# Eight places of a hand-written order and an earlier fetch for two chunks, in an RWKV-7 block followed by a squared-ReLU feed-forward layer

## The chip, the cores and the metric

The kernel runs on one core of a Trainium2 chip. The metric is the device time of one execution in microseconds, as the median of several runs. All products are in float32; the feed-forward weights arrive as 64-bit floats and are converted on the chip. The engines are TensorE (PE in the profile; PEld is its weight load), VectorE (DVE), ScalarE (ACT), GpSimd (POOL) and SyncE (SP), which only issues DMAs. "SPq", "ACTq" and "POOLq" are the queues from which the engines' sequencers issue.

## The reference

A linear recurrence over 768 time steps for 4 batches and 8 heads of 40 dimensions, and then a feed-forward layer over the 3072 tokens (320 to 2048 to 320):

```python
for t in range(S):
    y[:, :, t] = np.einsum('bhd,bhde->bhe', rt, state)
    Sa = np.einsum('bhde,bhe->bhd', state, at)
    state_decay = state * wt[:, :, None, :] - np.einsum('bhd,bhe->bhde', Sa, bt)
    state = state_decay + np.einsum('bhd,bhe->bhde', vt, kt)
...
x = attn_out.transpose(0, 2, 1, 3).reshape(B * S, H * D)
h = np.maximum(x @ w_in, 0.0)
return (h * h @ w_out).astype(np.float32)
```

## The kernel before

The 768 steps are cut into six pieces of 128, so with four batches there are 24 chunks, numbered 0 to 23; chunk i is piece i // 4 of batch i % 4. Chunk i needs the state left by chunk i - 4. Within a chunk the recurrence becomes matrix products and the inverse of a triangular matrix (I + N), built of a and b and the decays.

Each chunk passes through these stages:

- `early(i)`, in six steps: TensorE turns w, VectorE makes running products of it (the decays), TensorE turns b and a, VectorE scales them, TensorE multiplies them and ScalarE copies the result to the tile N. The decays go to `kept_e[i]` in device memory, N to `kept_q` or `kept_d` (what the solver reads), `kept_n` (its lower block) and, for chunks 0 to 13, `kept_m` (the two 32-row operands that join halves of an inverse).
- `take(u)` and `solving(u)`: GpSimd reads N back for a unit of one, two or four chunks (0; 1; 2-3; 4-5; 6-7; 8-9; 10-11; 12-13; 14-17; 18-21; 22-23) and solves for the inverse row by row; the result goes to `kept_t[u]`. The units up to 12-13 are "fine": they solve blocks of 32, and two 32x32 products join each pair of blocks to one of 64.
- `inverses(j)` fetches the inverse again (tile `blocks` for a fine unit, straight to T for the others), calls `arrive(j)` for N and, in a fine unit, the joins' operand (tile `spares`), and for a fine unit does the join in three further steps: VectorE turns `blocks`, TensorE multiplies with `spares`, ScalarE copies, TensorE multiplies again, ScalarE copies to T.
- `chain(i)`, in eight steps: the products with the state, with T and N, and the new state; this is the serial part. Its output is a block of tokens.
- The feed-forward layer works on two chunks' tokens at a time: `thirds` and `whole` (first product, then ScalarE's ReLU), `square` (VectorE), `make_quarter` (second product).

The schedule is written out by hand, and each engine runs its instructions in the order in which the program emits them. There are two parts. The opening is a list of words, taken one after the other (line 932): `e4.1` is step 1 of `early(4)`; `LA`, `LW`, `lk`, `lb`, `lr`, `lv` fetch a and b, w, k, b, r, v; `sE`, `sN` store decays and N; `K` and `S` take and solve a unit; `B`, `A`, `J` fetch a fine inverse, its N with the joins' operand, and do a step of the join; `D` fetches decays; `rv`, `mrv`, `k`, `a`, `kb`, `ds`, `ts` prepare a chunk; `x` begins a chain and `c` does its next step; `mv` gathers tokens; `th`, `wh`, `sq`, `q` are the feed-forward steps; `pa` and `pd` are halves of a step that converts weights (ScalarE and VectorE in turn); `W` fetches weights; and `f` with a number is filler: matmuls of the identity whose result nobody reads, that many 128x128 columns of them. `@a` and `@g` put a word's DMA on ScalarE's or GpSimd's queue; otherwise it is SyncE's.

The second part is a loop of slots 7 to 23. Slot i (`sorted_slot`) runs chunk i's chain, chunk i + 1's preparation with its inverse, and feed-forward steps; near its end `loads(i + 2)` fetches the decays, k and b of chunk i + 2, and for a chunk that is the later one of its unit (`soon`) starts `inverses` at once. For the first chunk of a fine pair, `inverses` is started at the head of the slot before its own, right behind the first `make_quarter`: its first step issues `blocks`, then `arrive`'s three DMAs. Chunks 8 and below are fetched in the opening.

`arrive` does nothing when N is already there, so a later call of `inverses` for the same chunk issues only `blocks`. Line 494 is the fetch of N, 498 that of the joins' operand, 513 that of `blocks`, 969 that of decays in the loop and 891 in the opening; 264 is the filler, 331 a turn, 87 any product, 372 to 381 the scans, 401 a copy of N, 532 and 539 the copies in a join, 561 a copy of the turned v, 658 those of `times_t` in the chain.

Of the kernel before, what the change touches and what calls it, by code (L numbers as in the profile page):

```python
# [17 lines left out]
def kernel(  # L18
# [42 lines left out]
    for h, d, n in ((6, 0, D), (7, 0, D), (5, HALF, D - HALF)):  # L61
        while n:
            j, row, room_ = free[at]
# [4 lines left out]
            d, n = d + m_, n - m_  # L68
# [23 lines left out]
    def new(name, shape, bufs):  # L92
        return work.tile(shape, FP32, tag=name, name=name, bufs=bufs)
# [7 lines left out]
    def tick():  # L101
        for entry in line:
            entry[0] -= 1
        while line and line[0][0] <= 0:
            line.pop(0)[1]()
# [12 lines left out]
    class Ring:  # L118
# [6 lines left out]
        def next(self):  # L125
            self.at = (self.at + 1) % len(self.tiles)
            return self.tiles[self.at]
# [15 lines left out]
    def fetch(ring, src, i):  # L143
        bb, c = order[i]
        t_ = rings[ring].next()
        on_queue[0].dma_start(out=t_[:, :, :D], in_=src[bb, :, c * C:(c + 1) * C, :].rearrange("h t d -> t h d"))
        return t_
# [168 lines left out]
    FINE = 8  # L316
# [3 lines left out]
    unit_of = {first + n: u for u, (first, nb) in enumerate(units) for n in range(nb)}  # L320
# [170 lines left out]
    def arrive(i, g, queue=nc.sync):  # L491
        if "N" not in g:
            g["N"] = new("N21", [HC, H, HC], 2)
            queue.dma_start(out=g["N"], in_=kept_n[i])
            if unit_of[i] < FINE:
                g["joins"] = spare("joins", i)
                for half in range(2):
                    queue.dma_start(out=g["joins"][half * HC:half * HC + Q], in_=kept_m[i][half, :, :, Q:])

    def inverses(i, g, queue=nc.sync, own_n=True):  # L500
        bb, c = order[i]
        u = unit_of[i]
        kept = kept_t[u][:, i - units[u][0]]
        g["T"] = T = new("T", [128, H, HC], 2)
        if u >= FINE:
            for col in range(classes(u)):
                queue.dma_start(out=T[col::classes(u)], in_=kept[col].rearrange("h f j t -> (f j) h t"))
        else:


            blocks = new("blocks", [128, H, Q], 1)
            for col in range(classes(u)):
                queue.dma_start(out=blocks[col::classes(u)], in_=kept[col].rearrange("h f k j t -> (f k j) h t"))
        if own_n:
            arrive(i, g, queue)
        if u >= FINE:
            return
        yield
        upper_ = spare("turned", i)
        nc.vector.transpose(upper_.rearrange("p h t -> p (h t)"), blocks.rearrange("p h t -> p (h t)"))  # L520
        for n in range(2):
            nc.scalar.activation(T[:, :, n * Q:(n + 1) * Q], blocks, Act.Copy, scale=which[:, n:n + 1])
        yield
        small = lambda: psum(ps_w)[:, :H * Q].rearrange("p (h t) -> p h t", h=H)
        p_ = small()
        mv = spare("mv", i)
        ends_ = [(slice(half * HC, half * HC + Q), slice(half * HC + Q, (half + 1) * HC)) for half in range(2)]
        for h in range(H):
            for one, two in ends_:
                mm(p_[two, h], g["joins"][one, h], upper_[one, h], True)  # L530
        for one, two in ends_:
            nc.scalar.copy(mv[two], p_[two])
        yield
        p_ = small()
        for h in range(H):
            for one, two in ends_:
                mm(p_[one, h], mv[two, h], blocks[two, h], True)
        for one, two in ends_:
            nc.scalar.copy(T[one, :, Q:], p_[one])
        yield  # L540


    soon = lambda i: i < 2 * B or unit_of[i - 1] == unit_of[i]
# [267 lines left out]
    def run(gen):  # L811
        for _ in gen:
            tick()
# [63 lines left out]
    def advance(u, n_):  # L877
        if u not in solves:
            solves[u] = [-1, solving(u, range(100), *((nc.vector, solved[:, Q * Q // 4:Q * Q // 2]) if u == 0 else ()))]
        while solves[u][0] < n_ and next(solves[u][1], "end") != "end":  # L880
            solves[u][0] += 1
        if n_ > 90:
            run(solves[u][1])
# [46 lines left out]
    }  # L930

    for word in """
e0.1 lv0 e0.2 e0.3 e0.4 e0.5 e1.1 e0.6 sN0 K0 LW2 e1.2 e1.3 e1.4 LA2 f3 e1.5 e1.6 sN1 K1 LW3 k0 a0 rv0 f2 e2.1 V0.10 V0.20 V0.31 f22 lk1 lv1 LA3 W0@g S1.8 mrv0 kb0 e2.2 e2.3 Z0 LW4 B0 e2.4 e3.1 x0 f10 e3.2 e2.5 sE2 e2.6 sN2 J0 e3.3 e3.4 J0 J0 e3.5 sE3 e3.6 sN3 c0 c0 c0 c0 c0 lv2 lr1 S1.20 c0 c0 LA4 S1.99 K2 B1 f3 W1 rv1 mrv1 lr2 f6 LW5 f4 e4.1 e4.2 e4.3 k1 kb1 e4.4 e4.5 W2@g LA5 sE4 pa0 lk2 pd0 D2 LW6 a1 e4.6 f5 pa1 pd1 x1 J1 pa2 pd2 W3 lv3 lb2 sN4 A2 pa3 pd3 rv2 f2 e5.1 e5.2 J1 f24 J1 f3 c1 LA6 S2.4 S2.99 f6 c1 mrv2 lr3 c1 f6 c1 e5.3 e5.4 e5.5 sE5@g f8 k2 c1 c1 c1 kb2 a2 pa4 e5.6 sN5@a pd4 pa5 pd5 e6.1 e6.2 x2 f30 e6.3 e6.4 B2 J2 K3 lk3 mv0 W4 A3 f10 e6.5 J2 J2 rv3 c2 c2 c2 e6.6 pa6 pd6 c2 mrv3 lb3 f9 LA7 D3 k3 pa7 B3 J3 LW7 c2 c2 kb3 lr4 sE6 J3 lv4 e7.1 pd7 pa8 c2 W5 lv5 lb4 a3 f8 lk4@a J3 e7.2 A4 rv4 W8 D4 sN6 S3.99 B4 W6 x3 W7 c3 pd8 c3 e7.3 pa9 pd9 mrv4 e7.4 e7.5 LA8 LW8 c3 pa10 J4 k4 sE7 pd10 W11 e7.6 c3 W10 lr5 c3 sN7 K4 S4.99 pa11 pd11 W12 kb4 ds4 J4 J4 pa12 pd12 c3 ts4 W9 f4 pa13 pd13 W13 a4 pa14 c3 D5 B5 mv1 pd14 e8.1 e8.2 f4 x4 lk5 W14 A5 LA9 c4 pa15 pd15 pa16 pd16 ds5 pa17 f10 rv5 pd17 f3 th0 J5 pa18 pd18 W15@a pa19 pd19 W16 lb5 mrv5 wh0 c4 pa20 pd20 pa21 lr6 c4 th0 wh0 e8.3 pd21 lv6 c4 e8.4 LA10 W17 e8.5 LW9 k5 kb5 c4 c4 e8.6 pa22 pd22 W19 sN8 th0 sE8 wh0 LW10 a5 J5 th0 wh0 sq0 W18@g pa23 ts5 c4 lk6 D6 e9.1 e9.2 A6 J5 e9.3 e9.4 e9.5 x5 lb6 B6 c5 f1 sq0 sE9@a pd23 W20 e9.6 sN9 K5 LW11 rv6 lv7 LA11 pa24 ds6 e10.1 e10.2 c5 pd24 pa25 mrv6 pd25 e10.3 k6 J6 pa26 pd26 c5 th0 wh0 e10.4 LA12 e10.5 sE10 lr7 c5 c5 th0 J6 kb6 c5 c5 e11.1 a6 ts6 e10.6 sN10 LW12 LW13 lk7@a e11.2 mv2 wh0 D7 e11.3 x6 e11.4 J6 q0 sq0 q0 e11.5 e12.1 e11.6 sN11@g S5.99 K6 S6.99 e12.2 sq0 e12.3 q0 q0 c6 B7 lb7 sE11 rv7 A7 wh0 q0 c6 mrv7 e12.4 q0 ds7 q0 J7 e12.5 sE12 c6 q0 k7 kb7 th0 sq0 c6 J7 c6 a7 c6 e12.6 LA13 lr8 LW14 e13.1 ts7 wh0 th0 th0 e13.2 e13.3 LA14 c6 wh0 sN12 lv8 e13.4 q0 A8 x7 J7 B8 e13.5 e13.6 sN13 q0 lb8 sq0 D8 sE13@g K7 S7.99 lk8
""".split():
        word, _, queue = word.partition("@")
        on_queue[0] = {"": nc.sync, "a": nc.scalar, "g": nc.gpsimd}[queue]
        kind = word.rstrip("0123456789.")
        at = word[len(kind):]
        if kind == "V":
            advance(0, int(at.split(".")[1]))  # L940
        elif kind == "Z":
            run(solves[0][1])
        elif kind == "S":
            advance(*(int(n_) for n_ in at.split(".")))
        else:
            kinds[kind](int(at.split(".")[0]))
        on_queue[0] = nc.sync
        tick()
# [11 lines left out]
    def fetch_next(i, *names):  # L960
        if i < len(order):
            to = ready[i]["x"] if "x" in ready.get(i, {}) else loaded.setdefault(i, {})
            to.update({nm: fetch(nm, {"k": k, "b": b, "r": r, "v": v}[nm], i) for nm in names if nm not in to})

    def loads(j):
        if j < len(order):
            n = ready.setdefault(j, {})
            n["dec"] = kept_here[j % 2]
            nc.sync.dma_start(out=n["dec"][:USED], in_=kept_e[j])
            fetch_next(j, "k", "b")  # L970
            if soon(j) and j > B:
                n["joining"] = inverses(j, n)
                next(n["joining"], None)
# [8 lines left out]
    def sorted_slot(i, g, ch):  # L982
# [41 lines left out]
        if more:  # L1024
            begin_chain(j, n)
        loads(j + 1)
        step(second.square, second.make_quarter, on(two), on(two))
        if i in ahead and len(ahead[i]) > 1:
# [5 lines left out]
    for i in range(LAID, len(order)):  # L1034
        tc.no_sync_barrier()
        g = ready.pop(i)
# [41 lines left out]
```

## Time and profile before

| What | us |
|---|---|
| median of 5 runs | 958.28 |
| the five runs | 950.44, 957.14, 958.28, 959.34, 964.04 |
| the profiled execution | 958.28 |
| its span | 956.6 |
| TensorE busy | 902.7 (94%) |
| VectorE, ScalarE, GpSimd busy | 466.9, 285.9, 510.1 |
| mean granted TensorE clock | 0.945 |

The clock row of the profile's slices, shown below, is in tenths of full speed; one slice is 23.9 us long. The opening ends near 332 us; slots 7, 8, 9, 10 and 11 begin near 332, 370, 407, 447 and 482 us. From slot 10 on TensorE is busy without gaps almost to the end. In the rows below, "<-" behind an idle time names what ended it. In rows of stretches a matmul counts as busy for as long as it takes, at whichever clock.

### The profile page before, as it was taken

To read this page: it belongs to the slowest core of one execution; us is meant where nothing else is said; L and a number is where in the kernel's file an instruction comes from. 1 tells how busy PE (TensorE), PEld (TensorE's weight loads), DVE (VectorE), ACT (ScalarE), POOL (GpSimd) and SP (SyncE) were. 2 spreads that over 40 slices of the span, in tenths; PEclk is the share of its full clock that TensorE was granted. 3 is DMA by queue.
4 is the path that set the end of the run, shared out by engine and by line. 5 is a ranking of instruction groups with operands and counts; after the bars stand their busy time and mean duration, and the time that the engine had idled before them with its cause. 6 is when DMAs were issued, how large, how long until landed. Compare 5 with 4: busy or idle time off the path is not lost.

```text
span 956.6 us, 22558 instructions
## 1 busy us (share of the span) xinstructions
PE 902.7 (94%) x9116; PEld 726.7 (76%) x9116; DVE 466.9 (49%) x1131; ACT 285.9 (30%) x735; POOL 510.1 (53%) x935
## 2 busy tenths in 40 slices
PE   6668989879999999989999999999999999999998
PEld 5456667668787887878888888887888878887775
DVE  5926647788863355543655454644334332231110
ACT  3033334544532343232333332222212222222111
POOL 4658356064008777229999849999768860000000
PEclk7767988589999999999999999999999999999999
DMA  9779878866868488994664786604564154120000
GB/s 111 123 148 154 172 124 184 185 133 134 178 103 167 84 153 153 166 166 92 117 94 86 123 177 113 113 18 84 124 122 75 35 108 79 40 34 10 12 14 15
DMA packets 253268, 103.38 MB, mean 108 GB/s; under 512 B 234155, under 2 KB 240299, under 8 KB 252011
## 3 DMA queue, kind: packets, MB, share of 16 engines
q1 hardware_dynamic: 244709, 83.00, 49.5%
q0 software_dynamic: 3760, 17.10, 7.3%
q10 hardware_dynamic: 4693, 1.83, 0.9%
q8 instruction: 72, 1.18, 0.6%
q14 instruction: 34, 0.27, 0.1%
HBM read 69.00 MB, written 30.92 MB: 104 GB/s over the span
## 4 chain that ended last, share of the span: by engine, by line
PE 81%; DVE 6%; DMA 6%; ACT 3%; POOL 2%; issue 1%; SPq 1%; ACTq 0%; POOLq 0%; DVEq 0%
PE ps_f L87 39%; PE ps_w L87 17%; PE ps_c L87 13%; PE ps_w L331 5%; PE ps_f L264 3%; DMA spares<-kept_m 2%; DMA dec<-kept_e 1%; PE ps_c L671 1%; PE ps_c L598 1%; PE ps_w L582 1%; DMA kept_q<-N 1%; DMA half_n<-kept_q 1%; ACT N L401 1%; DVE decay L381 1%; POOL half_t L480 1%
## 5 line engine op out<-in xcount | busy, mean ns | idle before, releaser
L478 POOL TENSOR_TENSOR half_p<-half_n,half_t 128x462 f32<-128x462 f32 (+39 forms) x406 | 221.7, 546 | 75.5 <-DMA half_n<-kept_q 23.4
L480 POOL TENSOR_TENSOR half_t<-half_t,half_p 128x462 f32<-128x462 f32 (+39 forms) x406 | 238.4, 587 | 31.8
L87 PE MATMUL ps_f<-w_out,hid 128*128 128x320 f32 x768 | 218.4, 436 | 0.0
L87 PEld LDWEIGHTS ps_f<-w_out,hid 128*128 128x128 f32 x768 | 142.1, 190 | 54.1 <-issue 0.2
L87 PE MATMUL ps_f<-tokens,w_in 128*128 128x256 f32 x672 | 156.6, 387 | 0.0
L87 PEld LDWEIGHTS ps_f<-tokens,w_in 128*128 128x128 f32 x672 | 125.9, 192 | 18.6 <-issue 1.9
L769 DVE TENSOR_TENSOR hid<-hid 128x512 f32<-128x512 f32 x96 | 81.7, 890 | 50.6 <-ACT hid L762 50.2
L762 ACT ACTIVATE hid<-ps_f 128x512 f32<-128x512 f32 x84 | 49.9, 597 | 80.9 <-PE ps_f L87 80.9
L697 DVE TENSOR_TENSOR tokens<-ps_c,dec 128x512 f32<-128x512 f32 x24 | 16.6, 692 | 86.4 <-PE ps_c L87 78.1
L451 POOL DMA_DIRECT2D half_n<-kept_q x18 | 9.4, 529 | 90.2 <-DMA kept_q<-N 47.8
L347 DVE TENSOR_TENSOR RX<-ps_w,upper 128x512 f32<-128x512 f32 x48 | 30.9, 685 | 50.3 <-PE ps_w L87 50.1
L372 DVE TENSOR_TENSOR_SCAN decay<-ps_w,ones 128x64 f32<-128x64 f32 x88 | 24.0, 273 | 60.9 <-PE ps_w L331 60.9
L264 PE MATMUL ps_f<-ident 128*128 128x512 f32 (+3 forms) x108 | 49.5, 592 | 0.0
L548 DVE TENSOR_TENSOR kvT<-ps_w,dec 128x512 f32<-128x512 f32 x24 | 16.5, 686 | 66.6 <-ACT minus_x L658 35.6
L347 DVE TENSOR_TENSOR RV<-ps_w,upper 128x512 f32<-128x512 f32 x48 | 30.9, 685 | 34.9 <-PE ps_w L87 34.7
L398 ACT COPY N<-ps_w 128x256 f32<-128x256 f32 x48 | 17.7, 368 | 100.3 <-PE ps_w L87 58.6
L87 PE MATMUL ps_f<-tokens,w_third 64*128 64x256 f32 x336 | 46.4, 387 | 0.1
L87 PEld LDWEIGHTS ps_c<-xr,T 64*64 64x64 f32 x768 | 28.9, 143 | 20.1 <-issue 14.3
L331 PE MATMUL ps_w<-ident,in_ab 128*128 128x128 f32 x184 | 27.9, 296 | 12.8 <-DVE RV L347 9.1
L570 DVE TENSOR_TENSOR f<-end,dec 128x4 f32<-128x4 f32 x20 | 5.7, 284 | 66.9 <-DMA dec<-kept_e 66.9
L87 PE MATMUL ps_c<-xr,T 64*64 64x40 f32 x768 | 34.9, 237 | 3.6 <-ACT xr L647 2.4
L560 ACT COPY rT<-ps_w 128x512 f32<-128x512 f32 x24 | 14.1, 586 | 80.6 <-PE ps_w L331 80.5
(151 smaller groups left out, 1469.4 us busy)
## 6 DMA issues: line engine op xcount, KB each, us to landing
dec<-kept_e SPq DMA_DIRECT2D x22, 633.8 KB
kept_e<-decay SPq DMA_DIRECT2D x19, 633.8 KB
in_w<-in_w_dram SPq DMA_DIRECT2D x24, 160.0 KB
in_b<-in_b_dram SPq DMA_DIRECT2D x24, 160.0 KB
in_ab<-in_a_dram SPq DMA_DIRECT2D x24, 160.0 KB
in_r<-in_r_dram SPq DMA_DIRECT2D x24, 160.0 KB
in_v<-in_v_dram SPq DMA_DIRECT2D x24, 160.0 KB
out_dram<-o SPq DMA_DIRECT2D x24, 160.0 KB
```

The source lines that it names most:

```text
L87: nc.tensor.matmul(o, l_, r_, start=start, stop=True, skip_group_check=True)
L264: nc.tensor.matmul(fill_bank[:, :n * 128], ident, ident.unsqueeze(1).to_broadcast([128, n, 128]), start=True, stop=True, skip_group_check= ...
L331: nc.tensor.transpose(p_[:, q * 128:(q + 1) * 128], pair(x_, q), ident)
L347: nc.vector.tensor_tensor(t_, p_, over4(upper), Alu.mult)
L372: nc.vector.tensor_tensor_scan(up[:, q, MID + 1:C + 1], wT[:, q, MID:], ones, 1.0, Alu.mult, Alu.mult)
L398: nc.scalar.copy(plain, p_[:, ::2].rearrange("s h (f t) -> s f h t", f=2))
L478: eng.tensor_tensor(p_, part[:, at:at + m_].unsqueeze(1).to_broadcast([128, n, m_]), t3[:, :n, s:s + 1].to_broadcast([128, n, m_]), Alu.mult)
L480: eng.tensor_tensor(t3[:, :n, s + 1:], t3[:, :n, s + 1:], p_, Alu.subtract)
L548: nc.vector.tensor_tensor(kT, kT_, down[:, :, 1:C + 1], Alu.mult)
L697: nc.vector.tensor_tensor(t_, y_, g["up"][:, :, :C], Alu.mult)
L762: nc.scalar.activation(h_, p_.rearrange("p f t -> p (f t)"), Act.Relu)
L769: nc.vector.tensor_tensor(h_, h_, h_, Alu.mult)
```

## The change

In the loop, `loads(j)` calls `arrive` for a chunk that is not the later one of its unit and whose unit is fine. In the list of the opening eight places are ordered anew; the words themselves are the same 477.

```diff
@@ loads(j) @@
             fetch_next(j, "k", "b")
+            if not soon(j) and unit_of[j] < FINE:
+                arrive(j, n)
             if soon(j) and j > B:
@@ the list of words, by place @@
-e3.2 e2.5 sE2 e2.6 sN2
+e3.2 e2.5 e2.6 sE2 sN2
...
-lr2 f6 LW5 f4 e4.1 e4.2 e4.3 k1 kb1 e4.4
+lr2 e4.1 e4.2 e4.3 k1 kb1 f6 LW5 f4 e4.4
...
-mrv2 lr3 c1 f6 c1 e5.3 e5.4 e5.5
+mrv2 lr3 f6 c1 e5.3 e5.4 c1 e5.5
...
-e7.6 c3 W10 lr5 c3 sN7
+e7.6 W10 lr5 c3 c3 sN7
...
-c3 ts4 W9 f4 pa13 pd13
+c3 pa13 ts4 W9 f4 pd13
...
-pa17 f10 rv5 pd17 f3 th0
+pa17 pd17 f3 rv5 f10 th0
...
-x5 lb6 B6 c5 f1 sq0 sE9@a pd23 W20
+x5 lb6 sE9@a pd23 B6 c5 f1 sq0 W20
...
-LW14 e13.1 ts7 wh0 th0 th0 e13.2 e13.3 LA14 c6 wh0 sN12 lv8 e13.4 q0 A8 x7 J7 B8 e13.5 e13.6 sN13
+LW14 wh0 th0 th0 e13.1 e13.2 e13.3 LA14 e13.4 e13.5 c6 wh0 sN12 ts7 lv8 q0 A8 e13.6 x7 J7 B8 sN13
```

More of the change, by code (lines that the diff above doesn't have):

```diff
@@ L932 @@
     for word in """
-e0.1 lv0 e0.2 e0.3 e0.4 e0.5 e1.1 e0.6 sN0 K0 LW2 e1.2 e1.3 e1.4 LA2 f3 e1.5 e1.6 sN1 K1 LW3 k0 a0 rv0 f2 e2.1 V0.10 V0.20 V0.31 f22 lk1 lv1 LA3 W0@g S1.8 mrv0 kb0 e2.2 e2.3 Z0 LW4 B0 e2.4 e3.1 x0 f10 e3.2 e2.5 sE2 e2.6 sN2 J0 e3.3 e3.4 J0 J0 e3.5 sE3 e3.6 sN3 c0 c0 c0 c0 c0 lv2 lr1 S1.20 c0 c0 LA4 S1.99 K2 B1 f3 W1 rv1 mrv1 lr2 f6 LW5 f4 e4.1 e4.2 e4.3 k1 kb1 e4.4 e4.5 W2@g LA5 sE4 pa0 lk2 pd0 D2 LW6 a1 e4.6 f5 pa1 pd1 x1 J1 pa2 pd2 W3 lv3 lb2 sN4 A2 pa3 pd3 rv2 f2 e5.1 e5.2 J1 f24 J1 f3 c1 LA6 S2.4 S2.99 f6 c1 mrv2 lr3 c1 f6 c1 e5.3 e5.4 e5.5 sE5@g f8 k2 c1 c1 c1 kb2 a2 pa4 e5.6 sN5@a pd4 pa5 pd5 e6.1 e6.2 x2 f30 e6.3 e6.4 B2 J2 K3 lk3 mv0 W4 A3 f10 e6.5 J2 J2 rv3 c2 c2 c2 e6.6 pa6 pd6 c2 mrv3 lb3 f9 LA7 D3 k3 pa7 B3 J3 LW7 c2 c2 kb3 lr4 sE6 J3 lv4 e7.1 pd7 pa8 c2 W5 lv5 lb4 a3 f8 lk4@a J3 e7.2 A4 rv4 W8 D4 sN6 S3.99 B4 W6 x3 W7 c3 pd8 c3 e7.3 pa9 pd9 mrv4 e7.4 e7.5 LA8 LW8 c3 pa10 J4 k4 sE7 pd10 W11 e7.6 c3 W10 lr5 c3 sN7 K4 S4.99 pa11 pd11 W12 kb4 ds4 J4 J4 pa12 pd12 c3 ts4 W9 f4 pa13 pd13 W13 a4 pa14 c3 D5 B5 mv1 pd14 e8.1 e8.2 f4 x4 lk5 W14 A5 LA9 c4 pa15 pd15 pa16 pd16 ds5 pa17 f10 rv5 pd17 f3 th0 J5 pa18 pd18 W15@a pa19 pd19 W16 lb5 mrv5 wh0 c4 pa20 pd20 pa21 lr6 c4 th0 wh0 e8.3 pd21 lv6 c4 e8.4 LA10 W17 e8.5 LW9 k5 kb5 c4 c4 e8.6 pa22 pd22 W19 sN8 th0 sE8 wh0 LW10 a5 J5 th0 wh0 sq0 W18@g pa23 ts5 c4 lk6 D6 e9.1 e9.2 A6 J5 e9.3 e9.4 e9.5 x5 lb6 B6 c5 f1 sq0 sE9@a pd23 W20 e9.6 sN9 K5 LW11 rv6 lv7 LA11 pa24 ds6 e10.1 e10.2 c5 pd24 pa25 mrv6 pd25 e10.3 k6 J6 pa26 pd26 c5 th0 wh0 e10.4 LA12 e10.5 sE10 lr7 c5 c5 th0 J6 kb6 c5 c5 e11.1 a6 ts6 e10.6 sN10 LW12 LW13 lk7@a e11.2 mv2 wh0 D7 e11.3 x6 e11.4 J6 q0 sq0 q0 e11.5 e12.1 e11.6 sN11@g S5.99 K6 S6.99 e12.2 sq0 e12.3 q0 q0 c6 B7 lb7 sE11 rv7 A7 wh0 q0 c6 mrv7 e12.4 q0 ds7 q0 J7 e12.5 sE12 c6 q0 k7 kb7 th0 sq0 c6 J7 c6 a7 c6 e12.6 LA13 lr8 LW14 e13.1 ts7 wh0 th0 th0 e13.2 e13.3 LA14 c6 wh0 sN12 lv8 e13.4 q0 A8 x7 J7 B8 e13.5 e13.6 sN13 q0 lb8 sq0 D8 sE13@g K7 S7.99 lk8
@@ new lines @@
+e0.1 lv0 e0.2 e0.3 e0.4 e0.5 e1.1 e0.6 sN0 K0 LW2 e1.2 e1.3 e1.4 LA2 f3 e1.5 e1.6 sN1 K1 LW3 k0 a0 rv0 f2 e2.1 V0.10 V0.20 V0.31 f22 lk1 lv1 LA3 W0@g S1.8 mrv0 kb0 e2.2 e2.3 Z0 LW4 B0 e2.4 e3.1 x0 f10 e3.2 e2.5 e2.6 sE2 sN2 J0 e3.3 e3.4 J0 J0 e3.5 sE3 e3.6 sN3 c0 c0 c0 c0 c0 lv2 lr1 S1.20 c0 c0 LA4 S1.99 K2 B1 f3 W1 rv1 mrv1 lr2 e4.1 e4.2 e4.3 k1 kb1 f6 LW5 f4 e4.4 e4.5 W2@g LA5 sE4 pa0 lk2 pd0 D2 LW6 a1 e4.6 f5 pa1 pd1 x1 J1 pa2 pd2 W3 lv3 lb2 sN4 A2 pa3 pd3 rv2 f2 e5.1 e5.2 J1 f24 J1 f3 c1 LA6 S2.4 S2.99 f6 c1 mrv2 lr3 f6 c1 e5.3 e5.4 c1 e5.5 sE5@g f8 k2 c1 c1 c1 kb2 a2 pa4 e5.6 sN5@a pd4 pa5 pd5 e6.1 e6.2 x2 f30 e6.3 e6.4 B2 J2 K3 lk3 mv0 W4 A3 f10 e6.5 J2 J2 rv3 c2 c2 c2 e6.6 pa6 pd6 c2 mrv3 lb3 f9 LA7 D3 k3 pa7 B3 J3 LW7 c2 c2 kb3 lr4 sE6 J3 lv4 e7.1 pd7 pa8 c2 W5 lv5 lb4 a3 f8 lk4@a J3 e7.2 A4 rv4 W8 D4 sN6 S3.99 B4 W6 x3 W7 c3 pd8 c3 e7.3 pa9 pd9 mrv4 e7.4 e7.5 LA8 LW8 c3 pa10 J4 k4 sE7 pd10 W11 e7.6 W10 lr5 c3 c3 sN7 K4 S4.99 pa11 pd11 W12 kb4 ds4 J4 J4 pa12 pd12 c3 pa13 ts4 W9 f4 pd13 W13 a4 pa14 c3 D5 B5 mv1 pd14 e8.1 e8.2 f4 x4 lk5 W14 A5 LA9 c4 pa15 pd15 pa16 pd16 ds5 pa17 pd17 f3 rv5 f10 th0 J5 pa18 pd18 W15@a pa19 pd19 W16 lb5 mrv5 wh0 c4 pa20 pd20 pa21 lr6 c4 th0 wh0 e8.3 pd21 lv6 c4 e8.4 LA10 W17 e8.5 LW9 k5 kb5 c4 c4 e8.6 pa22 pd22 W19 sN8 th0 sE8 wh0 LW10 a5 J5 th0 wh0 sq0 W18@g pa23 ts5 c4 lk6 D6 e9.1 e9.2 A6 J5 e9.3 e9.4 e9.5 x5 lb6 sE9@a pd23 B6 c5 f1 sq0 W20 e9.6 sN9 K5 LW11 rv6 lv7 LA11 pa24 ds6 e10.1 e10.2 c5 pd24 pa25 mrv6 pd25 e10.3 k6 J6 pa26 pd26 c5 th0 wh0 e10.4 LA12 e10.5 sE10 lr7 c5 c5 th0 J6 kb6 c5 c5 e11.1 a6 ts6 e10.6 sN10 LW12 LW13 lk7@a e11.2 mv2 wh0 D7 e11.3 x6 e11.4 J6 q0 sq0 q0 e11.5 e12.1 e11.6 sN11@g S5.99 K6 S6.99 e12.2 sq0 e12.3 q0 q0 c6 B7 lb7 sE11 rv7 A7 wh0 q0 c6 mrv7 e12.4 q0 ds7 q0 J7 e12.5 sE12 c6 q0 k7 kb7 th0 sq0 c6 J7 c6 a7 c6 e12.6 LA13 lr8 LW14 wh0 th0 th0 e13.1 e13.2 e13.3 LA14 e13.4 e13.5 c6 wh0 sN12 ts7 lv8 q0 A8 e13.6 x7 J7 B8 sN13 q0 lb8 sq0 D8 sE13@g K7 S7.99 lk8
```

## The prediction

> **What bounds the kernel now.** I read the page first, then the granted clock by stretches, then the chain of waits, and last the timelines of TensorE and of SyncE's queue around each edited place. The profiled execution took 958.28 us, which is also the median of the five runs; 956.6 us of it are span and 1.7 us lie around it. The sums below are made against it.
>
> ```profile
> span 956.6 us, 22558 instructions
> ...
> PE 902.7 (94%) x9116; PEld 726.7 (76%) x9116; DVE 466.9 (49%) x1131; ACT 285.9 (30%) x735; POOL 510.1 (53%) x935
> ...
> PEclk7767988589999999999999999999999999999999
> ```
>
> TensorE is busy for 94%, so only two things can be won: its 54 us of gaps, and the stretches in which its clock is not granted in full. The clock row shows both where they are: in the first nine slices (the opening), and nowhere else except for a little near slice 18. Stretches cut at the loop's slots (slot i joins chunk i; columns are the length, then busy time of each engine, then granted clock, DMA share and GB/s) put that little into slot 9:
>
> ```profile
> 407.15:447.38 40.23, 37.79 (x418) 31.76 (x412) 16.65 (x40) 13.26 (x38) 22.58 (x35) 0.92 0.66 125
> 447.38:481.66 34.28, 34.28 (x419) 28.77 (x413) 18.80 (x40) 11.56 (x31) 32.00 (x30) 1.00 0.78 127
> 481.66:515.93 34.27, 34.27 (x417) 28.75 (x413) 19.25 (x40) 11.55 (x31) 32.07 (x29) 1.00 0.41 72
> ```
>
> Slots 9 and 11 carry the same kinds of work (both start the fine inverse of an even chunk in their own slot), yet slot 9 is 40.23 - 34.27 = 5.96 us longer: 40.23 - 37.79 = 2.44 us of gaps, and 37.79 - 34.27 = 3.52 us of the same matmuls running slower. The chain of waits and TensorE's timeline name the gap:
>
> ```profile
> 415.12 0.59 SPq L498
> ...
> 415.76 10.51 DMA spares<-kept_m
> ```
> ```profile
> 422.60 1.06 PE L87 MATMUL ps_c<-rT,sd 128*128 128x128 f32 x8
> 426.01 0.99 PE L87 MATMUL ps_w<-spares 32*32 32x32 f32 x32 [2.35 <-DMA spares<-kept_m]
> ```
>
> The joins' operand of chunk 10 was issued at 415.12, beside 1.5 MB of GpSimd's own fetch (two transfers of 768 KB, issued at 414.78), and landed 10.5 us later. And the gap costs more than itself:
>
> ```profile
> 424.22:427.63 3.41, 1.53 (x44) 1.41 (x46) 0.46 (x2) 0.58 (x2) 1.59 (x5) 1.00 1.47 135
> 427.63:431.04 3.41, 3.41 (x32) 3.24 (x30) 2.19 (x4) 0.15 (x1) 2.91 (x7) 0.50 1.26 230
> 431.04:434.46 3.42, 3.42 (x25) 3.02 (x24) 1.97 (x3) 0.84 (x3) 3.11 (x5) 0.50 0.19 75
> 434.46:437.87 3.41, 3.41 (x17) 2.80 (x16) 0.00 (x0) 2.40 (x8) 3.10 (x5) 1.00 0.27 54
> ```
>
> After the stretch with 1.53 us of work the clock is 0.50 for two stretches of 3.41 us; a full half of 6.83 us is 3.4 us, about the 3.52 found above.
>
> **The loop's edit, step by step.** `loads(j)` now calls `arrive` for a chunk that heads a fine pair. Of the chunks it sees (9 and on) these are 10 and 12, so three DMAs each (128 KB of N, two of 32 KB for the joins) move: from the head of slot 9 to the tail of slot 8, and from slot 11's head to slot 10's tail. Only SyncE issues them; they pass its queue behind b, and are gone behind the blocks. Is there room?
>
> ```profile
> 399.95 0.67 SPq L146 DMA_DIRECT2D in_b<-in_b_dram  x1
> 405.41 1.60 SPq L110 DMA_DIRECT2D kept_e<-decay  x1
> ```
>
> The three issues took 0.62 + 1.25 us in slot 9; the queue stands idle from 400.62 to 405.41, because the next store waits for VectorE. So they end near 402.5 and cost nothing there; without that idle stretch they would hold up the store, and what follows it, by 1.9 us. The two buffers they fill were last read by chunk 8, in slots 7 and 8, so no wait is added. Issued near 400.6, even with the 10.5 us of before they land by 412, and TensorE asks at 423.66. The pieces that come next in the order (r, v, blocks) are the ones that slot 11 runs without a gap, and the blocks had landed by 416.79, when ScalarE used them. I take slot 9 at slot 11's length: -6.0 us. Bounds: 0, if the blocks or another piece of the 1.5 MB crowd is late instead, and -6.0, since nothing else is in the slot. For chunk 12 there is no gap to close (slot 11 is busy for all of 34.27 us): 0.
>
> [...]
>
> What the gain runs into later: GpSimd's solves keep their own time. The inverse of chunks 18 to 21 is fetched at 693.03, as soon as it is stored, and chunk 18 first uses it at 714.39; 7.6 us less work before it leaves 13 us. Hidden.
>
> **The opening's words.** Eight edits; most move a word past words of other engines, so that each engine's own order stays. One reorders an engine where it waits: `f6 LW5 f4` goes behind `e4.1 e4.2 e4.3 k1 kb1`.
>
> ```profile
> 76.74 2.42 PE L264 MATMUL ps_f<-ident 128*128 128x512 f32 x6
> 78.99 0.60 PE L331 MATMUL ps_w<-ident,in_w 128*128 128x128 f32 x4
> ...
> 83.56 0.63 PE L331 MATMUL ps_w<-ident,in_ab 128*128 128x128 f32 x4 [2.67 <-DVE decay L381]
> ```
>
> The 2.42 us of filler run first, then w's turn, and VectorE's scans of it start at 79.63 though VectorE is free at 78.06. With w's turn first they start 1.57 us earlier, all that follows on VectorE to 88.97 with them, and TensorE's gap before a's turn shrinks from 2.67 to 1.1 us: its own work up to there is the same, and the bank that it waits for comes free 1.57 us earlier. LW5's DMA has the same neighbours on SyncE. I take -1.6 us. This gap too is followed by a slow clock:
>
> ```profile
> 82.88:86.30 3.42, 2.36 (x22) 1.89 (x24) 3.42 (x9) 0.00 (x0) 2.90 (x7) 1.00 1.06 182
> 86.30:89.71 3.41, 3.41 (x18) 2.25 (x17) 2.61 (x5) 1.58 (x6) 2.94 (x7) 0.50 0.91 111
> ...
> 96.54:99.95 3.41, 3.41 (x22) 1.69 (x19) 2.50 (x5) 1.32 (x3) 2.94 (x7) 1.00 1.01 180
> ```
>
> 10.24 us at half: if the clock then holds, up to 5.1 us more. Bounds 0 (eaten by the next wait, TensorE's 2.02 us for VectorE at 133.81) and -6.7. I leave the 5.1 out of the sum, since gaps far smaller than 2 us (1.23 and 1.09 us at 165 and 172) stand beside a halved clock as well.
>
> The rest at nothing, each with its cover. `e2.6` before `sE2`, and `c3` behind `W10 lr5`: no engine's order changes. `c1` behind `f6` and then behind `e5.4`: TensorE has the same work there, and no gap from 96.5 to 113.6; the transposition of x loses its filler of 1.56 us and gets 1.04 us of turns ahead of it instead, against the 0.60 us of ScalarE's copies that it waits for; without that cover, 0.6 us. `pa13` before `ts4`: ScalarE waits for VectorE until 185.66 and copies the turned state 1.6 us later; it is read at 222.94. `f10 rv5` behind `pd17 f3`: the gap of 3.92 us at 206.46 waits for ScalarE's copy, which stands behind the rounding pair that ended at 205.3; both orders leave that. `sE9@a pd23` before `B6 c5`: see the last rival. Slot 6's `wh0 th0 th0` before `e13.1`, with `e13.4 e13.5` earlier and `ts7` later: TensorE is busy for 31.83 of the 32 us from 300 on, a and b of 13 were issued by 305.0 and are now turned near 316 instead of 323.3, so even the joins' 10.5 us to land would do; later still, each us is one of TensorE's.
>
> Sum: 958.3 - 6.0 - 1.6 = 950.7 us.
>
> **Rivals.** (1) The opening's clock holds after 86.3: 950.7 - 5.1 = 945.6. For it: the stretch with the gap goes from 1.43 to about 3 us of work; against it: VectorE idles only 2.1 us up to 91.08, so TensorE would soon wait for it. (2) The gain is mostly hidden: another piece of the crowd halves slot 9's clock, or only the 2.4 us gap goes and the opening's 1.6 are eaten: 955.9. For it: DMA engines are 96% busy in slot 8, where the DMAs now go; against it: 23 us of lead. That the edit reaches no chunk at all would be 958.3; chunk 10 meets its condition, so I give this nothing of its own. (3) Slower: `sE9@a` now stands before c5's copies on ScalarE, which is held until VectorE ends at 247.46 and the issue is done. At 0.57 us, as it took at 247.54, the copies end just before 248.75, when the next work starts anyway. But SyncE's issue at that moment took 5.83 us (blocks, 244.65); at 5.83 the copies of N begin at 253.9, TensorE's wait at 250 grows by 5.1 us, and a halved clock of 10.24 us adds 5.1: 950.7 + 10.2 = 960.9. It beats the gains from an issue of 3.2 us on (ScalarE's fetch of k at 159.43 took 3.27).
>
> **How the numbers follow.** Forecast 0.47, rival 1 0.27, rival 2 0.16, rival 3 0.06, something unseen 0.04. The five runs lie between 950.4 and 964.0, so 1% (9.6 us, to 948.7 and 967.9) is about what can be told from no change. Faster by over 1%: three quarters of rival 1 and, with a few us of scatter, about two fifths of the forecast, 0.39. Slower by over 1%: part of rival 3 and of the unseen, 0.06. Within: 0.55. The range takes in rival 1 with scatter below it and rival 2 above: 942 to 958.
>
> **What would show it.** Slot 9 at 34.3 us with a clock of 1.00 and the joins' issue in slot 8; TensorE's gap before the turn of a near 82 at 1.1 us; whether the clock is 0.50 after it. Wrong: a wait for blocks or r in slot 9; ScalarE held near 247; an opening that ends no earlier.

## The result and the profile after

| | median us | runs |
|---|---|---|
| before | 957.14 (947.26 to 967.05) | 95 |
| after | 952.37 (946.43 to 959.64) | 53 |

The ratio after to before is 0.9968, 95% interval [0.9955, 0.9981]: a gain of 3.1 us of 957, between 1.8 and 4.3. It compares means, 956.1 and 953.0 us, without the five runs of before that took over 1.5% longer than its fastest; the medians lie 4.8 us apart. The forecast was a gain of 7.6 us. The time lies inside the range and within 1% of before, the likeliest case; but the sum had 7.6 us where 3.1 were measured. The profiled execution of after took 950.01 us, so this one pair of profiles shows 8.3 us between them. The experiments show why that is no measure: one execution of before is one draw from a wide scatter.

The page of after, the lines that answer to those of before:

```profile
span 948.3 us, 22557 instructions
...
PE 893.6 (94%) x9116; PEld 717.2 (76%) x9116; DVE 464.9 (49%) x1131; ACT 285.5 (30%) x735; POOL 509.4 (54%) x935
...
PEclk9769978789899999999999999999999999999999
```

The little loss near slice 18 is gone; the opening still has its low digits, in other slices than before. Cut at slots 9 and 11 of after (length, busy times, granted clock, DMA share, GB/s):

```profile
405.02:439.30 34.28, 34.28 (x419) 28.76 (x413) 15.81 (x40) 13.17 (x38) 15.59 (x27) 1.00 0.78 147
...
473.57:507.85 34.28, 34.28 (x418) 28.76 (x413) 18.87 (x40) 11.56 (x31) 32.17 (x28) 1.00 0.44 73
```

Slot 9 now has slot 11's length, with TensorE busy for all of it at full clock, as forecast. TensorE's timeline of after, where before waited 2.35 us for the joins' operand, and the SyncE queue's:

```profile
420.46 1.06 PE L87 MATMUL ps_c<-rT,sd 128*128 128x128 f32 x8
421.45 0.69 PE L87 MATMUL ps_w<-spares 32*32 32x32 f32 x32
```
```profile
398.03 1.82 SPq L146 DMA_DIRECT2D in_b<-in_b_dram  x1
400.21 5.20 SPq L494 DMA_DIRECT2D N<-kept_n  x1
405.48 1.24 SPq L498 DMA_DIRECT2D spares<-kept_m  x2
406.82 0.51 SPq L110 DMA_DIRECT2D kept_e<-decay  x1
```

The operand is issued at 405.48, 16 us ahead of its use. But the fetch of N, 0.62 us in slot 9 of before, now takes 5.20 us to issue. ("Backlog" below means just this: an issue that takes several us instead of about 0.6.) The store of the decays behind it, which went out at 405.41 in before and took 1.60 us, goes out at 406.82. Counted from chunk 10's turn of the decays (line 582), at 422.2 us in before and 420.0 in after, it goes out 13.2 us ahead instead of 16.7. So the move holds SyncE's queue up by 3.5 us; it is free all the same, since TensorE has no gap in slot 9.

In the opening, TensorE's timeline of after behind the filler that was moved:

```profile
78.37 0.60 PE L331 MATMUL ps_w<-ident,in_ab 128*128 128x128 f32 x4
80.02 0.63 PE L331 MATMUL ps_w<-ident,in_ab 128*128 128x128 f32 x4 [1.05 <-issue]
...
88.17 0.60 PE L331 MATMUL ps_w<-ident,in_w 128*128 128x128 f32 x4
90.99 0.91 PE L87 MATMUL ps_w<-spares 32*32 32x32 f32 x32 [2.22 <-DVE spares L520]
```

The gap of 2.67 us before a's turn is 1.05, as forecast (1.1). A new one of 2.22 us stands 11 us later: VectorE's turn of chunk 1's `blocks` (line 520) starts at 90.41, behind five steps of the weights' conversion. Stretches of after around it:

```profile
87.93:91.35 3.42, 1.20 (x27) 0.89 (x28) 2.87 (x6) 1.31 (x4) 2.95 (x7) 0.99 1.00 241
91.35:94.76 3.41, 3.41 (x25) 1.80 (x20) 3.31 (x5) 0.49 (x1) 3.02 (x6) 0.51 0.95 224
```

Again a short stretch of work (1.20 us) is followed by half the clock: one stretch now, three in before.

### The profile page after: what moved, and what is told of

It reads as the page before. It is cut to its first block, busy times and chain, and to the rows that moved or that the text cites. A ratio compares the mean times of both kernels' runs of the same rounds, so it can differ in the third digit from the quotient of the medians.

```text
span 948.3 us, 22557 instructions
## 1 busy us (share of the span) xinstructions
PE 893.6 (94%) x9116; PEld 717.2 (76%) x9116; DVE 464.9 (49%) x1131; ACT 285.5 (30%) x735; POOL 509.4 (54%) x935
## 4 chain that ended last, share of the span: by engine, by line
PE 80%; DVE 8%; DMA 4%; ACT 4%; issue 3%; POOL 0%; SPq 0%; ACTq 0%; DVEq 0%; POOLq 0%
PE ps_f L87 41%; PE ps_w L87 16%; PE ps_c L87 13%; PE ps_w L331 5%; PE ps_f L264 2%; PE ps_c L598 1%; PE ps_c L671 1%; PE ps_w L582 1%; DMA hid<-in_moe_w_in_dram 1%; DMA kept_q<-N 1%; DMA dec<-kept_e 1%; DVE decay L381 1%; ACT N L401 1%; DVE half_t L478 1%; DVE half_t L480 1%
## 5 line engine op out<-in xcount | busy, mean ns | idle before, releaser
L87 PE MATMUL ps_f<-tokens,w_in 128*128 128x256 f32 x672 | 158.9, 391 | 0.0
L451 POOL DMA_DIRECT2D half_n<-kept_q x18 | 9.4, 528 | 84.3 <-DMA kept_q<-N 44.7
```

Source lines behind the costliest of these rows:

```text
L87: nc.tensor.matmul(o, l_, r_, start=start, stop=True, skip_group_check=True)
```

## The experiments

The theory after the result: the gain is slot 9's alone; it is smaller than 6.0 us because the profile of before happened to be an execution in which slot 9 lost a lot; and the words of the opening win at one place what they lose at later ones. The rivals: that slot 9's loss is the same in every execution and the words (or the moved DMAs) give some 3 us back; and that the words carry part of the gain.

From slot 10 on all 20 profiles are alike: from chunk 11's turn of the decays to chunk 23's it is 382.06 to 382.10 us in each. So nearly every difference lies ahead of chunk 11's turn, and I cut each profile at the turns of the decays (line 582), one per chunk. "Slot 9" below is from chunk 10's turn to chunk 11's. Ratios are to before, run alongside on the same chip.

**The loop's edit alone**, with the old list of words:

```diff
             fetch_next(j, "k", "b")
+            if not soon(j) and unit_of[j] < FINE:
+                arrive(j, n)
```

> The order of the opening as before, only the earlier fetch for chunks 10 and 12. Theory A (the gap in slot 9 is there in every execution, and costs 6 us; the reordered opening gives some of it back): slot 9 at 34.3 us, the median 6 us under before, about 0.994. Theory B (gap or halved clock in slot 9 come in only a part of the executions of before, by where the 3.41 us windows of the clock fall): slot 9 at 34.3 us here too, but the median only 3 to 4 us under before, 0.996 to 0.997, and the slow end of before's times thinned out.

Measured: 0.9932 [0.9901, 0.9963], median 950.46, slot 9 34.3 us. Once more on another chip:

> The earlier fetch alone, in the same rounds as the changed kernel. If the reordered opening gives part of the gain back (theory A): 2 to 3 us faster than the changed kernel. If the earlier fetch is all there is on average and the first 6.5 us were chance (theory B): equal to the changed kernel within 1.5 us.

Measured: 0.9991 [0.9955, 1.0026], median 952.41, slot 9 34.3 us. The two intervals hardly overlap; the ratios average 0.996, which is -3.7 us, good to about 2.3 either way. Slot 9 is as long in both profiles, so what varies is before and the opening.

**The words alone**, with the old `loads`:

```diff
@@ the list of words: all eight places as in the change @@
```

> The new order of the opening, the loop's fetch as before. Theory A: the opening is 2 to 3 us slower than before, so 1.002 to 1.003, with slot 9 at 40 us in the profile. Theory B: the opening gains what the profile of the changed kernel shows up to chunk 4 (about 1 us), so 0.998 to 1.000, with slot 9 at 40 us or less by execution.

Measured: 0.9986 [0.9954, 1.0018], median 955.57. And again:

> The new order of the opening alone, timed again and for a second profile. If the order moves only the phase (shorter by 2.8 us up to chunk 2, given back near 250 us in those executions in which the same four gaps there halve the clock): within 2 us of before, 0.998 to 1.001. If it is a gain of its own: 0.997 or under. Slot 9: a gap of 1 us or more if the gap does not depend on the opening, none if the new order itself removes it.

Measured: 0.9983 [0.9949, 1.0016], median 955.05. Each interval holds 1; the words are worth 1.5 us at the most likely, good to about 2.2 either way, so no effect is possible too; that they give some 3 us back is not. The profiles were worth more than the times: slot 9, with the old fetch in both, is 34.3 us in the first and 41.4 in the second.

**The kernels unchanged, profiled again.** After:

> The changed kernel once more, for a second profile. Both theories: slot 9 at 34.3 us at full clock. A time near 951 us goes with the halved stretches of its first profile; a time near 957 us should show one or two more of them in the opening, 3 to 7 us in sum.

> The changed kernel, on the same chip and in the same rounds as the three below. All theories: 3 to 4 us under before, slot 9 at 34.3 us.

> The changed kernel in the same rounds, for comparison: 0.9955 to 0.998 of before.

Measured: 948.12 in a single execution; then 0.9957 [0.9925, 0.9989] and 0.9949 [0.9921, 0.9977]. Before:

> The kernel before once more, for a second profile. Theory A: slot 9 is 40.2 us again with a gap near 2.4 us and 6.8 us at half clock. Theory B: the gap is again there, but slot 9 can be 34.3 to 40 us, according to where the windows fall; a time near 951 us would go with a short one.

> The kernel before, for one more profile of slot 9. If the joins' operand keeps TensorE waiting in every execution and always halves the clock: slot 9 at 40.2 us. If the wait comes and goes with SyncE's backlog and the windows of the clock: anything from 34.3 to 40.2 us, the mean of all profiles near 37.5.

> As the run ahead of it: 40.2 us if slot 9's loss is fixed, 34.3 to 40.2 us if it comes and goes.

> As the two runs ahead of it: 40.2 us if slot 9's loss is fixed, 34.3 to 40.2 us if it comes and goes.

Measured, one execution each: 953.34, 954.14, 946.77 and 953.25. These profiles give the size of slot 9's term. The table takes all profiles with the old fetch, and how long before chunk 10's turn the joins' operand was issued. A half clock is one of 0.50:

| profile | issued ahead by, us | gap for it, us | half clock after it, us | slot 9, us |
|---|---|---|---|---|
| before_fourth | 8.9 | 0 | 0 | 34.3 |
| words_alone | 8.6 | 0 | 0 | 34.3 |
| before_again | 8.0 | 1.53 | 0 | 36.0 |
| before | 7.0 | 2.35 | 6.8 | 40.2 |
| words_second | 5.8 | 3.50 | 6.8 | 41.4 |
| before_fifth | 5.6 | 3.74 | 10.2 | 42.4 |
| before_third | 4.7 | 4.36 | 6.8 | 42.1 |
| any of 12 with the early fetch (after: 14.5) | | 0 | 0 | 34.3 |

Mean with the old fetch: 38.7 us (standard error 1.4). So the edit wins 4.4 us on average in these profiles, not 6.0, and in two of the seven nothing. What sets the lead is how long SyncE's issues take: in all seven the store of the decays goes out 16.7 us ahead of chunk 10's turn, and the operand follows it by 7.9 to 12.1 us with the same issues between. TensorE and the queue in before_fourth:

```profile
417.05 1.06 PE L87 MATMUL ps_c<-rT,sd 128*128 128x128 f32 x8
418.04 0.69 PE L87 MATMUL ps_w<-spares 32*32 32x32 f32 x32
```
```profile
399.87 0.37 SPq L110 DMA_DIRECT2D kept_e<-decay  x1
...
407.73 1.34 SPq L498 DMA_DIRECT2D spares<-kept_m  x2
```

and in before_third:

```profile
416.74 0.94 PE L87 MATMUL ps_c<-rT,sd 128*128 128x128 f32 x7
422.05 1.38 PE L87 MATMUL ps_w<-spares 32*32 32x32 f32 x32 [4.36 <-DMA spares<-kept_m]
```
```profile
399.45 4.58 SPq L110 DMA_DIRECT2D kept_e<-decay  x1
404.14 4.67 SPq L110 DMA_DIRECT2D kept_d<-N  x4
...
411.54 1.57 SPq L498 DMA_DIRECT2D spares<-kept_m  x2
```

The same program: the store of the decays takes 0.37 us to issue in one execution and 4.58 in the other, the operand goes out 4 us later, and TensorE stands for 4.36 us.

GpSimd's 1.5 MB come into it as well. In before GpSimd's first operation on them is

```profile
425.69 0.29 POOL L478 TENSOR_TENSOR half_p<-half_n,half_t 128x63 f32<-128x63 f32 x1 [7.65 <-DMA half_n<-kept_d]
```

and TensorE's product with the operand starts 0.32 us later, at 426.01. In all five profiles with a gap it starts 0.3 to 0.4 us behind GpSimd: in these the small operand is there only when the large fetch is.

**The fetch made later**, as the opposite dose: N and the operand of chunks 10 and 12 go behind w, b, a and r of the same slot.

```diff
-        joining = n.pop("joining") if early_join else inverses(j, n) if more else iter(())
+        joining = n.pop("joining") if early_join else inverses(j, n, own_n=unit_of[j] >= FINE) if more else iter(())
...
         fetch_next(j + 1, "r")
+        if fine and not early_join:
+            arrive(j, n)
```

> The kernel before, with N and the joins' operand of chunks 10 and 12 fetched later instead of earlier: behind w, b, a and r of the same slot. If the gap in slot 9 is the joins' operand waiting in the crowd of GpSimd's 1.5 MB: they are issued near 426 there instead of 415, the gap grows from 1.5 to 2.4 us to about 5 us, the clock is halved each time, slot 9 takes 43 to 45 us, and the time is 4 us or more above before (1.004 or more). Slot 11, which has the same later fetch but no crowd, stays at 34.3 us. If the gap comes from elsewhere: slot 9 at 36 to 40 us as before.

Measured: 1.0071 [1.0042, 1.0101], median 960.07: slower than before, by 6.8 us. TensorE's timeline, SyncE's, and the stretches of slots 9 and 11:

```profile
430.98 1.15 PE L87 MATMUL ps_w<-spares 32*32 32x32 f32 x32 [6.40 <-DMA spares<-kept_m]
```
```profile
420.65 6.55 SPq L494 DMA_DIRECT2D N<-kept_n  x1
427.25 1.26 SPq L498 DMA_DIRECT2D spares<-kept_m  x2
```
```profile
408.08:451.76 43.68, 37.28 (x418) 31.50 (x412) 16.74 (x40) 13.18 (x38) 24.25 (x37) 0.88 0.59 114
...
486.03:520.30 34.27, 34.27 (x420) 28.80 (x412) 19.35 (x40) 11.54 (x31) 32.15 (x28) 1.00 0.42 72
```

Slot 9 loses 43.68 - 34.27 = 9.4 us: 6.40 of gap, and 3.0 of half clock (10.2 us of it, 3.9 of them within the gap). Slot 11 has its fetch at the same place of the program and loses nothing:

```profile
491.67 1.25 SPq L498 DMA_DIRECT2D spares<-kept_m  x2
```
```profile
502.50 0.69 PE L87 MATMUL ps_w<-spares 32*32 32x32 f32 x32
```

There N's issue takes 1.17 us, the operand is issued 10.8 us ahead of its product, and the DMA share is 0.42 against 0.59. In slot 9 it goes out at 427.25, behind 6.55 us for N, when TensorE has stood since 424.58. What costs is the wait for the operand, and the place in the program does not set it alone.

**The early fetch with the filler's place alone**, the other seven places as in before:

```diff
-lr2 f6 LW5 f4 e4.1 e4.2 e4.3 k1 kb1 e4.4
+lr2 e4.1 e4.2 e4.3 k1 kb1 f6 LW5 f4 e4.4
```

> The earlier fetch and, of the eight places in the opening, only the filler moved behind the turns of w, k and the decays. In the two profiles of the changed kernel and the one of its words alone the opening is 2.2 us shorter between the turns of decays of chunks 0 and 2 than in three without them. If the filler is all of that: the same 84.3 us here instead of 86.5, and a time 1.5 to 2 us under the earlier fetch alone. If another of the eight places is behind it: 86.5 us here.

Measured: 0.9962 [0.9935, 0.9989], median 949.96. All profiles together, cut by stretch (means in us of 9 profiles with the old place and 11 with the new; the variants of the join below left out of the second row, 8 and 8):

| from the turn of chunk's decays to | old filler | moved filler | difference |
|---|---|---|---|
| 0 to 2 | 87.1 | 84.3 | -2.8 |
| 2 to 3 | 35.2 | 37.0 | +1.8 |
| 5 to 6 | 41.1 | 42.3 | +1.2 |

This kernel has 84.6 us in the first stretch, so the filler's move is enough for the gain there, and the other seven places show nothing. How much of it lasts is open. Of the 1.8 us in the second row 0.8 is a longer wait before the join of chunk 2 (next experiment) and 1.0 lies behind it, where the clock is halved for 17.1 us in all 8 profiles with the moved filler and in 5 of 8 with the old one. The third row rests on 5 of the 11 (last section). From chunk 0's turn to chunk 10's, without the variants of the join, it is 390.0 us with the old words and 389.4 with the new: 0.7 us less, with a standard error of 1.3.

**Taking the loss back.** The gap between chunks 2 and 3 is a join's step that waits for VectorE. ScalarE's and VectorE's timelines of after say why VectorE is late:

```profile
118.72 0.31 ACTq L420 DMA_DIRECT2D kept_q<-N  x1
...
122.17 0.51 ACTq L420 DMA_DIRECT2D kept_n<-N  x1
122.72 0.76 ACT L275 ACTIVATE hid<-hid,lowest 128x512 int32<-128x512 int32 x1 [3.47 <-DMA kept_q<-N]
```
```profile
123.52 0.69 DVE L284 SCALAR_TENSOR_TENSOR hid<-hid 128x512 int32<-128x512 int32 x1 [3.52 <-ACT hid L275]
```

VectorE has stood for 3.52 us, waiting for ScalarE's half of the weights' conversion (line 275), and that starts when ScalarE's queue has issued the seven stores of chunk 5's N (`sN5@a`): 0.04 or 0.05 us behind the last issue in all 20 profiles. Behind it come VectorE's half, the scans of `e6.2` and then the turn for the join. In the 16 profiles with the join in its old place ScalarE stands for 2.9 to 4.5 us here, and in 15 of them TensorE's gap is 1.0 to 1.1 us shorter than that; the gap is 2.1 us on average with the old filler and 2.9 with the moved one. No run takes the stores off ScalarE's queue; the run below moves the turn ahead of the scans, that is, ahead of chunk 6's second step:

```diff
-e6.1 e6.2 x2 f30 e6.3 e6.4 B2 J2 K3 lk3
+e6.1 B2 J2 e6.2 x2 f30 e6.3 e6.4 K3 lk3
```

> The changed kernel, with B2 and the first J2 ahead of e6.2 (VectorE turns the blocks of chunk 2 before the scans of chunk 6; no other engine but ScalarE changes order, by one pair). It takes away the gap of 2.0 to 2.4 us at 131, which every profile has, and behind which the clock is halved for up to 17 us. If a gap of this size costs itself alone: the stretch between the turns of decays of chunks 2 and 3 goes from 37 to 35 us, the time 2 us under the changed kernel, 0.994 to 0.995 of before. If the clock makes most of the cost: the stretch goes to 32 us or less, the half clock between 132 and 150 is gone or short, 0.988 to 0.992. If the gain is again given back later: 0.996.

> The changed kernel with B2 and the first J2 ahead of e6.2 once more, now in the same rounds as the changed kernel itself. Its first profile had the gap of 2.2 us gone and three of 0.7 to 0.9 us in its place, the clock still halved for 13.7 us, and the stretch between chunks 2 and 3 at 34.7 us. If that is a gain that lasts: 2 to 3 us under the changed kernel again. If its 0.9929 was chance: equal to it.

Measured (with all of the change): 0.9929 [0.9902, 0.9955] and 0.9926 [0.9897, 0.9955], medians 947.36 and 948.72. TensorE's timeline in after:

```profile
130.82 0.69 PE L87 MATMUL ps_w<-spares 32*32 32x32 f32 x32 [2.41 <-DVE spares L520]
131.97 1.44 PE L87 MATMUL ps_w<-blocks,spares 32*32 32x32 f32 x32 [0.45 <-ACT spares L532]
```

and in join2_first:

```profile
131.57 0.69 PE L87 MATMUL ps_w<-blocks,spares 32*32 32x32 f32 x32 [0.85 <-ACT spares L532]
133.15 0.66 PE L331 MATMUL ps_w<-ident,in_r 128*128 128x128 f32 x4 [0.89 <-ACT T L539]
134.48 1.12 PE L331 MATMUL ps_w<-ident,in_v 128*128 128x128 f32 x4 [0.68 <-ACT rT L560]
```

The gap for VectorE is gone, three smaller ones for ScalarE stand in its place, and the half clock stays (13.7 us from 134.5, after 17.1). The stretch from 2 to 3 is 34.8 and 34.7 us instead of 37.0: about the gap itself, no more. The same edit with the old words and the early fetch:

> The earlier fetch and the earlier J2, with the opening's old order otherwise. If the eight places are worth nothing on average (the theory so far): equal to join2_second within 1.5 us, though its stretch up to chunk 2 is 86.5 us or more and not 84.3. If they gain what they gain up to chunk 2: 2 to 3 us slower than join2_second.

Measured: 0.9948 [0.9917, 0.9979], median 950.98, which is 2.3 us above join2_second (2.1 by the ratios): the second of the two outcomes. Its stretch from 0 to 2 is 86.5 us against 84.6 there, that from 2 to 3 34.6. So with the join moved the words may well be worth the 1.6 us of the forecast; the intervals overlap, so it is not shown.

**Another gap of the opening**: 3.45 us at 200 us in after, before a product that waits for a copy on ScalarE. `rv5` ahead of the rounding pair:

```diff
-ds5 pa17 pd17 f3 rv5 f10 th0
+ds5 rv5 pa17 pd17 f3 f10 th0
```

> The changed kernel, with rv5 ahead of pa17, so that ScalarE copies r and v of chunk 5 before the rounding pair and not behind it. It takes away the gap of 3.5 to 3.9 us at 202 to 206 and the 6.8 us of half clock behind it. Gap alone: 3.5 us less between the turns of decays of chunks 4 and 5 (42.8 to 39.3). Gap and clock: 6 to 7 us less. In time: 0.992 or 0.990 of before. If VectorE and ScalarE, which alternate on the weights there, bound the stretch: under 1 us less, 0.996.

Measured: 0.9957 [0.9928, 0.9986], median 950.91, no better than after. The stretch from 4 to 5 takes 45.0 us here against 43.0 in after. The gap is not gone, it is elsewhere:

```profile
197.29 1.16 PE L87 MATMUL ps_w<-rT,kvT 40*128 40x128 f32 x16 [0.53 <-ACT kvT L561]
207.21 1.38 PE L87 MATMUL ps_c<-xr,T 64*64 64x40 f32 x16 [4.51 <-ACT xr L665]
```

Both edits together:

> Both of these edits on the changed kernel. If gaps and their clock are what the opening loses: 8 us or more under the changed kernel, 0.985 to 0.990 of before. If what one stretch gains is given back by the next: no faster than the better of the two alone.

Measured: 0.9932 [0.9903, 0.996], median 947.95; the join's gain and nothing besides. The best version is the one with the join moved: run side by side on one chip its median was 948.72 against after's 949.43, and its ratios, 0.9929 and 0.9926, are below all of after's (0.9968, 0.9957, 0.9949). The intervals overlap, so that it beats before is shown, and that it beats after is likely.

## Why the prediction was right and wrong, point by point

**Slot 9, "I take slot 9 at slot 11's length: -6.0 us".** This step failed, in its size. The mechanism held in every run: with the early fetch slot 9 is 34.3 us in 12 of 12 profiles, and a later fetch makes it 43.7. What the step subtracted from was wrong. It took the 40.23 us of one execution for the kernel's, and in seven profiles the length runs from 34.3 to 42.4 with a mean of 38.7, so the term is -4.4 with a standard error of 1.4. The mean alone does not rule out -6.0; the times of the loop's edit alone, -3.7 give or take 2.3, also point below it. The execution of 958.28 us that all sums start from was itself 2.2 us slower than the mean of before. The prediction stated that the operand was issued at 415.12 and did not ask what set that time; SyncE's queue in the same profile had two issues that took 5.83 us together, beside ones of 0.6, a sign that such times vary.

**"They end near 402.5 and cost nothing there".** The result held, the working did not. N's issue alone takes 4.4 to 6.0 us in the 12 profiles with the early fetch (5.20 in after), so the idle stretch of SyncE is used up whole. The prediction priced the hold-up of the next store, without that stretch, at 1.9 us; it is 1.4 to 3.6 us, counted from chunk 10's turn. It costs TensorE nothing, for a reason that the prediction did not give: the store and what follows it have slack, and slot 9 has no gap.

**The rest of the loop.** The operand is there when TensorE asks, nothing else of the crowd is late, chunk 12 gains nothing (34.28 in slot 11), all as stated. GpSimd's solves stay hidden: chunk 10's turn comes anywhere from 415 to 425 us, and what follows takes the same 382 us each time.

**The filler, "-1.6 us".** Not shown, and not refuted. The gap came out as worked out (1.05 us in after against 1.1), and the stretch up to chunk 2 even won 2.8 us. Up to chunk 10 the profiles leave 0.7 of it, with a standard error of 1.3; the times of the words alone say 1.5, give or take 2.2. The bound "0 (eaten by the next wait, TensorE's 2.02 us for VectorE at 133.81)" named the right place, but that wait takes back 0.8 us of the 2.8, not all; VectorE is late there because it waits for ScalarE, which is busy issuing stores. The two terms as the profiles give them, -4.4 and -0.7, make -5.1; the measured -3.1 [-4.3, -1.8] is 2.0 away, about the error of the two together (1.9). So the runs cannot say how much of the shortfall is slot 9's and how much the filler's.

**The other seven places at nothing.** No profile shows an effect of theirs above the scatter. `pd17 f3` ahead of `rv5` left its gap (3.92 us in before, 3.45 in after), as stated.

**The rivals.** Rival 1, the opening's clock holds after 86.3: the clock did, the time did not follow. Between 75 and 130 us the clock is halved for 0 to 3.4 us in the 11 profiles with the moved filler and for 10.2 to 13.7 in the 9 with the old one; yet the stretch won 2.8 us and not 6.7, as its "against" said: TensorE soon waits for VectorE (the row at 90.99). Over the whole execution half clock is 77.4 us in after against 107.7 in before, but other executions of before have 74.2 to 85.0. Rival 2, 955.9, had the smaller gain by two mechanisms: another late piece of the crowd (did not come) or the opening's 1.6 us eaten (open, see above); the gain of 3.1 us lies near its 2.4, but not for its reasons, since slot 9 ran at full clock. Rival 3, ScalarE held by the store at `sE9@a`: no trace of it; the store's issue took 0.57 us in after as in before, and the four gaps of TensorE behind it (0.59, 0.50, 0.29 and 0.82 us) are the same in both.

**The half clock behind a gap.** The sum has 3.52 us for it in slot 9, beside 2.44 us of gaps. The gap of 2.35 us was followed by 6.8 us of half clock, that of 2.22 us at 90.99 in after by 3.4, and that of 1.53 us in before_again by none. So the gap that the sum starts from cost more than itself, and the one of 1.53 us did not.

**Open.** Whether the eight places together are worth 0 or 1.5 us; what makes an issue on SyncE take 0.4 us in one execution and 4.6 in the next; and why the stretch from 5 to 6 is longer with the moved filler in some executions only (see the last section).

## What to carry to other kernels

A term that subtracts one execution's wait needs a second execution: look at what sets the moment of issue, and if that is a queue with a backlog, take the mean over several profiles before pricing its removal. A gap that is closed early in a kernel is not yet time won at its end: here 2.8 us up to chunk 2 were 0.7, give or take 1.3, by chunk 10. And a load that moves on a queue costs the issue time of its new place: N's fetch took 0.62 us at the old one and 4.4 to 6.0 at the new.

## What the hardware showed that I had not expected

**The issue of one DMA on SyncE takes from 0.27 to several us**: 0.27 to 5.98 in before and 0.27 to 5.65 in after, 0.59 in the median of each, and 6.55 for N at 420.65 in fetch_later; the same instruction at the same place took 0.37 in one execution and 4.58 in another. Behind a long issue the next was short in some places (6.55 us for N, then 1.26 for two; 5.20 for N, then 1.24 for two) and long in others (in after 4.34 for a at 415.36, then 5.13 for r). What makes the long ones is not shown.

**The small operand lands late beside the crowd.** Two transfers of 32 KB took 10.5 us beside GpSimd's 1.5 MB. In the run with the late fetch, issued 1 us before GpSimd went on with its data (428.23), they took no more than 3.7 us from issue (427.25) to the product that waited for them (430.98).

**The same gaps are followed by half the clock in one execution and not in another.** The first two of these gaps near 240 us stand in every profile, all four in 13 of 20; here in after:

```profile
240.42 0.66 PE L87 MATMUL ps_c<-xr,T 64*64 64x40 f32 x16 [0.59 <-ACT xr L647]
242.00 1.16 PE L87 MATMUL ps_w<-decay,bT 40*128 40x128 f32 x16 [0.50 <-DVE decay L388]
244.47 0.66 PE L331 MATMUL ps_w<-ident,in_w 128*128 128x128 f32 x4 [0.29 <-ACT N L402]
246.55 1.16 PE L87 MATMUL ps_w<-rT,kvT 40*128 40x128 f32 x16 [0.82 <-ACT kvT L561]
```

In after they are followed by half clock (stretches of 3.41 us):

```profile
244.90:248.31 3.41, 2.59 (x41) 2.02 (x40) 2.79 (x11) 2.99 (x9) 0.00 (x0) 0.99 0.84 229
248.31:251.72 3.41, 3.41 (x25) 2.51 (x26) 3.31 (x8) 1.76 (x4) 0.55 (x2) 0.50 0.53 108
```

and in a second profile of after, with the gaps 1.75 us later, not:

```profile
243.11:246.52 3.41, 2.62 (x29) 2.13 (x28) 3.24 (x9) 2.06 (x8) 0.00 (x0) 1.00 1.18 190
246.52:249.94 3.42, 2.60 (x40) 2.05 (x38) 2.71 (x11) 3.11 (x9) 0.00 (x0) 1.00 0.82 230
```

The stretch from 5 to 6 is 43.8 us in the one and 40.7 in the other. In the traces of before and after every period at half clock lasts a whole multiple of 3.41 us, one to seven of them (the last is cut off by the end): 13.65, 10.24, 17.07, 10.24, 17.07, 23.89 and 6.83 twice in before, 10.24, 17.07, 3.41, 17.07, 13.65 and 6.83 twice in after. Counted from the span's start in such steps, all of them begin 0.97 us past a step in before and 2.51 in after. What decides is not shown: the stretch ahead of the half clock holds 2.59 us of work, and the one like it that kept the full clock 2.60. With the moved filler 5 of 11 profiles have a long stretch there (43.6 to 45.7), with the old one none of 9; too few to call it an effect of the change. Counted from the first entry of a profile's clock, 7.5 to 27 us in, half clock adds up to 74 to 108 us of some 950, and over the 20 profiles it goes with the span at a correlation of 0.76.
